# Linear attention beside a gated feed-forward block: activation loads split and reordered, one mean subtracted by ScalarE, first transposes copied in halves, warm-up matmuls on a constant

## The chip, the cores and the metric

The kernel runs on one core of one Trainium2 chip. The metric is the time of one execution on the device in microseconds (us). Lower is better. Engines are named as in the profile: PE is TensorE, ACT is ScalarE, DVE is VectorE, POOL is GpSimd, and SP is SyncE, which issues the DMA transfers here.

## The reference

The input x has 2048 rows (tokens) of 512 columns in bfloat16. It is normalised per row (mean and variance, no scale or shift), and two branches of the result are added to it:

```python
xn = _layernorm(x)
# A: linear attention, H = 32 heads of 16
q, k, v = split(xn @ wqkv)
phi = lambda z: concat(softmax(z @ w_phi), softmax(-(z @ w_phi)))   # per head, 32 features
kv, z = phi(k)^T v, sum over tokens of phi(k)
A = ((phi(q) kv) / (phi(q) z + 1e-6)) @ wo
# B: gated feed-forward, 1792 hidden
B = ((xn @ w_gate) * (xn @ w_up)) @ w_down
out = x + A + B
```

## The kernel before, in words

The tokens are worked in 16 tiles of 128 rows. SBUF is one array, `arena`, in which names are offsets; PSUM is one array, `ps`, with eight banks of 512 float32 columns.

Each tile of x is centred, transposed so that the 512 columns lie on partitions in four quarters (`xnT`, quarter q), and multiplied by the value weights (`k_pe`) and the key and query weights. The key and query weights are first folded with `w_phi` into `Wp` (`wprime`), for which they are loaded transposed by a DMA (`load_wT`). The feed-forward block is worked in units of 128 hidden columns by 512 tokens (`glu`): four matmuls for the gate, four for the up part, a copy of the gate by ACT and a product by DVE. These units have low priority and fill PE's time between the steps of the attention. At the end `final` multiplies by `w_down` and `wo`, adds x and stores.

**Order of the work.** The code records steps with what they read and write. A list planner (`_order`) then sets the order on each engine from costs and due times written into the code: a DMA has an `at`, the time in ns at which its data counts as landed. Among steps that could start, the earliest goes first, and at equal times the one with the lower number. A step marked `urgent` is taken ahead of others if it can start within a grace (50 ns on PE, 300 ns elsewhere). `_emit_all` writes this fixed order into the engines' queues with semaphore waits. Each queue is worked in order: a step that waits holds up what stands behind it.

**The first 16 us**, where the edit lies. The first four tiles (`RAW = 4`) are only centred before their transpose; their scale is applied later. For each of them:

- `emit_centred(t)` finds the mean and subtracts it. Tiles 0, 2 and 3 do this on DVE: BATCH_NORM_STATS2 (L415), BATCH_NORM_AGGREGATE (L416), subtraction (L430). Tile 1 is in `ACT_MEAN`: its mean comes from an ACT activation with an accumulated sum (L423), and the subtraction stays on DVE (L430). Its variance is found later.
- `emit_T(t)` transposes the tile by four matmuls against the identity into one bank and copies the bank to `xnT` by one ACT activation (`act_op`, L277).
- `emit_root(t)` works the row's scale on POOL.
- `k_pe(t)` multiplies by the value weights: four matmuls of 512 columns, one for each quarter q. They are separate steps for the first four tiles. Quarters 0 and 1 need the first half of the value weights, 2 and 3 the second.

All matmuls are recorded at one line (L297), all plain DMA issues at L165, DMA transposes at L164, and PSUM copies by ACT at L277.

Loads at the start are issued by SP in this order: x tile 0, x tile 1, x tiles 2 and 3 in one transfer, the two halves of the value weights, gate and up weights (first four units), `w_phi`, x tiles 4 to 7, the transposed key weights, and more gate and up weights.

Before the first data is there, PE runs 27 matmuls on a block of zeros that DVE has written (L368, L369) into a bank that nothing reads, and four more behind tile 1's transpose.

Of the kernel before, what the change touches and what calls it, by code (L numbers as in the profile page):

```python
# [5 lines left out]
BF16 = mybir.dt.bfloat16  # L6
F32 = mybir.dt.float32
ACTF = mybir.ActivationFunctionType
# [4 lines left out]
PE, ACT, DVE, POOL, SP = "PE", "ACT", "DVE", "POOL", "SP"  # L13
# [7 lines left out]
NQ = D // 128  # L21
# [160 lines left out]
def bass_parallel_sum__linear_kernel_hedgehog__glu_gated_bilinear__prompt_kernel(  # L182
    nc: bass.Bass,
    A_x: bass.AP,
    A_wqkv: bass.AP,
    A_w_phi: bass.AP,
    A_wo: bass.AP,
    B_x: bass.AP,
    B_w_gate: bass.AP,
    B_w_up: bass.AP,  # L190
    B_w_down: bass.AP,
    out: bass.AP,
):
    with ExitStack() as es:
        _build(nc, es, A_x, A_wqkv, A_w_phi, A_wo, B_w_gate, B_w_up, B_w_down, out)


def _build(nc, es, A_x, A_wqkv, A_w_phi, A_wo, B_w_gate, B_w_up, B_w_down, out):
# [59 lines left out]
    def sbv(name, lo, n):  # L258
        off = layout[name] + lo
        return arena[:, off:off + n]  # L260

    def sbf(name, lo_f32, n_f32):
        off = layout[name]
        return arena[:, off:off + 2 * (lo_f32 + n_f32)].bitcast(F32)[:, lo_f32:lo_f32 + n_f32]

    def bank(b, lo=0, n=512):
        return psum[:, b * 512 + lo: b * 512 + lo + n]

    sc = _Sched(nc)


    def act_op(out_ap, in_ap, func=ACTF.Copy, scale=1.0, bias=None, prio=None):
        def fn(e):
            kw = {}
            if bias is not None:
                kw["bias"] = bias
            return e.activation(out=out_ap, in_=in_ap, func=func, scale=scale, **kw)  # L277
        r = [in_ap]
        if isinstance(scale, bass.AP):
            r.append(scale)  # L280
        if isinstance(bias, bass.AP):
            r.append(bias)
        return sc.step(ACT, fn, reads=r, writes=[out_ap], cost=(50.0 if str(in_ap.tensor.name) == "ps" else 95.0) + 0.833 * in_ap.free_size(),
                       lat=180.0, prio=prio)

    def dve(fn, reads, writes, n, rate=1.0, fixed=65.0, prio=None):
        return sc.step(DVE, fn, reads=reads, writes=writes, cost=fixed + rate * n / 0.96, lat=150.0, prio=prio)
# [4 lines left out]
    def mms(items, prio=None, cold=False):  # L292

        def fn(e):
            ins = None
            for o, l, r, a, z in items:
                ins = e.matmul(o, lhsT=l, rhs=r, start=a, stop=z)  # L297
            return ins
        reads = []
        writes = []  # L300
        c = 0.0
        for o, l, r, a, z in items:
            reads += [l, r]
            writes.append(o)
            c += max(25.0, o.free_size() / 2.4 + 2.3) * (1.92 if cold else 1.0)
        return sc.step(PE, fn, reads=reads, writes=writes, cost=c, lat=260.0, prio=prio)
# [12 lines left out]
    def x_tile(t):  # L319
        return sbv("x", t * 512, 512)  # L320

    xnT_v = sbv("xnT", 0, NQ * S_TOK).rearrange("p (q s) -> p q s", q=NQ)
# [5 lines left out]
    wv_v = sbv("wv", 0, NQ * 512).rearrange("p (q j) -> p q j", q=NQ)  # L328
# [7 lines left out]
    def load_x(on, t0, n, at):  # L336
        return sc.dma(on, sbv("x", t0 * 512, n * 512).rearrange("p (t d) -> p t d", t=n),
                      x_flat[t0 * 128:(t0 + n) * 128, :].rearrange("(t p) d -> p t d", p=128), at=at)

    def load_w(on, dst, src, at, issue=500.0):  # L340
        return sc.dma(on, dst, src, at=at, issue=issue)
# [5 lines left out]
    def load_gu(on, f0, n, at):  # L347
        return [load_w(on, v[:, :, f0 * 128:(f0 + n) * 128],
                       src[:, f0 * 128:(f0 + n) * 128].rearrange("(q p) f -> p q f", p=128), at)
                for v, src in ((wg_v, B_w_gate), (wu_v, B_w_up))]  # L350

    load_x(SP, 0, 1, 2950.0)
    load_x(SP, 1, 1, 3400.0)
    load_x(SP, 2, 2, 4700.0)
    wv_loads = [load_w(on, wv_v[:, 2 * h:2 * h + 2, :],
                       A_wqkv[h * 256:(h + 1) * 256, 1024:1536].rearrange("(q p) j -> p q j", p=128), at)
                for on, h, at in ((SP, 0, 5700.0), (SP, 1, 6600.0))]
    load_gu(SP, 0, 4, 9300.0)
    sc.dma(SP, wphi_v, bass.AP(tensor=A_w_phi.tensor, offset=A_w_phi.offset, ap=[[16, 128], [2048, NQ], [1, 16]]),
           at=10900.0)  # L360
# [3 lines left out]
    load_gu(SP, 9, 5, 22300.0)  # L364


    zero = sbv("tree", 0, 128)
    dve(lambda e: e.memset(zero, 0.0), [], [zero], 128)  # L368
    mms([(bank(7, 0, 128), zero, zero, True, True)] * 27, cold=True)  # L369


    def c_fn(e):
# [30 lines left out]
    mv_v = sbf("mv", 0, NT * 2).rearrange("p (t k) -> p t k", t=NT)  # L403
# [10 lines left out]
    def emit_moments(t):  # L414
        dve(lambda e: e.bn_stats(stats_v[:, t, 0:6], x_tile(t)), [x_tile(t)], [stats_v[:, t, 0:6]], 512)  # L415
        dve(lambda e: e.bn_aggr(mv_v[:, t, :], stats_v[:, t, 0:6]), [stats_v[:, t, 0:6]], [mv_v[:, t, :]], 6)  # L416

    def emit_centred(t):

        reads = [x_tile(t)]  # L420
        if t in ACT_MEAN:
            mean = lnt_v[:, 2, 8 + t:9 + t]
            sc.step(ACT, lambda e: e.activation(out=xn_tile(t), in_=x_tile(t), func=ACTF.Copy, scale=1.0 / 512.0,  # L423
                                                accum_out=mean),
                    reads=[x_tile(t)], writes=[xn_tile(t), mean], cost=720.0, lat=180.0)
            reads.append(xn_tile(t))
        else:
            mean = mv_v[:, t, 0:1]
            emit_moments(t)
        dve(lambda e: e.tensor_scalar(out=xn_tile(t), in0=x_tile(t), scalar1=mean, scalar2=None,  # L430
                                      op0=ALU.subtract), reads + [mean], [xn_tile(t)], 512, rate=0.5)

# [3 lines left out]
    def emit_root(t):  # L436
        pool(lambda e: e.tensor_scalar(out=veps(t), in0=mv_v[:, t, 1:2], scalar1=1e-5, scalar2=None, op0=ALU.add),
             [mv_v[:, t, :]], [veps(t)], 1)
        pool(lambda e: e.tensor_tensor(out=rstd_v[:, t, 0:1], in0=veps(t), in1=mhalf[:, 0:1], op=ALU.pow),
             [veps(t), mhalf], [rstd_v[:, t, 0:1]], 1, rate=155.0, fixed=400.0)  # L440
# [22 lines left out]
    def xn_tile(t):  # L463
        return sbv("xn", (t % 4) * 512, 512)
# [4 lines left out]
    def next_a():  # L469
        b = a_bank[0] % a_banks[0]  # L470
        a_bank[0] += 1
        return b

    def emit_T(t):
        b = (5, 6, 7, 4)[t] if t < RAW else next_a()
        mms([(bank(b, q * 128, 128), xn_tile(t)[:, q * 128:(q + 1) * 128], ident, True, True) for q in range(NQ)],
            cold=t < 2)
        act_op(xnT_v[:, :, t * 128:(t + 1) * 128], bank(b).rearrange("p (q s) -> p q s", q=NQ))

    def emit_xn(t):  # L480
        dve(lambda e: e.tensor_scalar(out=xn_tile(t), in0=x_tile(t), scalar1=mv_v[:, t, 0:1],  # L481
                                      scalar2=rstd_v[:, t, 0:1], op0=ALU.subtract, op1=ALU.mult),
            [x_tile(t), mv_v[:, t, 0:1], rstd_v[:, t, 0:1]], [xn_tile(t)], 512, rate=0.5)
        if t >= 4:
            sc.dma(SP, xnT_v[:, :, t * 128:(t + 1) * 128], xn_tile(t), transpose=True, issue=1250.0, land=3200.0,
                   at=36000.0 + 1300.0 * (t - 8) if t >= 8 else 23600.0 + 550.0 * (t - 4))
            return
        emit_T(t)
# [63 lines left out]
    def k_pe(t):  # L552
        b = next_a()
        items = group(bank(b), [(xnT(q, t * 128, 128), wv_v[:, q, :]) for q in range(NQ)])
        if t < RAW:
            for item in items:
                mms([item])
        else:
            mms(items)
        act_op(vext_all[:, t, :, 0:64], bank(b).rearrange("p (c j) -> p c j", c=8), scale=scale_of(t))  # L560
# [166 lines left out]
    for t in range(RAW):  # L727
        first = len(sc.steps)
        emit_centred(t)
        emit_T(t)  # L730
        for st in sc.steps[first:]:
            st.urgent = True
        if t == 1:
            mms([(bank(7, 0, 128), zero, zero, True, True)] * 4, cold=True).deps.append(sc.by_eng[PE][-2])
        if t in ACT_MEAN:
            emit_moments(t)
        emit_root(t)
        k_pe(t)
# [192 lines left out]
```

## Time and profile before

| What | Value |
|---|---|
| Median of 3 runs | 219.8 us (219.64 to 220.88) |
| The profiled execution | 219.75 us |
| Its span (first to last instruction) | 218.5 us |
| PE busy | 213.9 us, 98% of the span |
| DVE busy | 193.0 us, 88% |
| ACT busy | 115.8 us, 53% |
| POOL busy | 10.7 us, 5% |
| DMA packets' share of 16 engines | 40.4% |

The span leaves out what lies around the instructions, 1.25 us here. A busy PE need not be at its peak, since matmuls are pipelined and the profile models their ends. From one matmul's start to the next one's start is the measure of its pace. Idle time of an engine that does not set the end costs nothing.

### The profile page before, as it was taken

The numbers are of one execution on the slowest core, as the hardware profiler recorded it, in microseconds if no ns is written. First come the engines' busy times: TensorE is split into PE (matmuls) and PEld (weight loads), VectorE is DVE, ScalarE is ACT, GpSimd is POOL, SyncE is SP. The second block draws the span as 40 slices with busy tenths as digits, with TensorE's granted clock in tenths as the row PEclk, the third lists the DMA queues.
The fourth block names the chain that finished last, engine by engine and source line by source line (L and its number), as shares of the span: only waits on it lengthen the run. The fifth ranks groups of instructions, "written<-read, shape, count | busy, mean of one in ns | idle before, by whom it ended". The sixth has DMA issues, their size and how long they took to land.

```text
span 218.5 us, 3596 instructions
## 1 busy us (share of the span) xinstructions
PE 213.9 (98%) x1290; PEld 105.0 (48%) x1313; DVE 193.0 (88%) x549; ACT 115.8 (53%) x191; POOL 10.7 (5%) x29
## 2 busy tenths in 40 slices
PE   7999999999999999999999999999999999999996
PEld 7444444444445544444445544444544444454454
DVE  4577999999999389999998899999999999999532
ACT  4658987538443599965553687553444353121000
POOL 4532000010002000000000000000000000000000
DMA  6999540025900440000000002273456548546931
GB/s 172 316 238 354 100 172 4 0 52 147 329 3 13 85 99 0 0 0 3 0 0 1 3 0 48 48 99 74 96 116 128 106 110 106 123 111 126 139 76 48
DMA packets 47458, 19.91 MB, mean 91 GB/s; under 512 B 37456, under 2 KB 47440, under 8 KB 47440
## 3 DMA queue, kind: packets, MB, share of 16 engines
q1 hardware_dynamic: 47440, 19.69, 40.4%
q8 instruction: 10, 0.16, 0.3%
q14 instruction: 8, 0.07, 0.1%
HBM read 8.67 MB, written 2.10 MB: 49 GB/s over the span
## 4 chain that ended last, share of the span: by engine, by line
PE 95%; DMA 2%; issue 1%; SPq 1%; ACT 1%; DVE 0%
PE ps L297 95%; DMA arena<-in_A_wqkv_dram 2%; SPq L165 1%; ACT arena L277 1%; DVE arena L703 0%
## 5 line engine op out<-in xcount | busy, mean ns | idle before, releaser
L297 PE MATMUL ps<-arena 128*128 128x512 bf16 (+4 forms) x1290 | 213.9, 327 | 2.8 <-DVE arena L368 1.0
L297 PEld LDWEIGHTS ps<-arena 128*128 128x128 bf16 (+1 forms) x1313 | 105.0, 99 | 111.5 <-issue 1.1
L277 ACT ACTIVATE arena<-ps 128x512 bf16<-128x512 f32 (+1 forms) x136 | 71.8, 583 | 47.1 <-PE ps L297 40.2
L277 ACT ACTIVATE arena<-arena 128x1024 bf16<-128x1024 bf16 (+1 forms) x40 | 38.5, 977 | 30.1 <-DVE arena L528 29.9
L542 DVE TENSOR_TENSOR arena<-arena 128x512 f32<-128x512 bf16 (+3 forms) x128 | 48.8, 392 | 0.2
L598 DVE TENSOR_TENSOR arena<-ps,arena 128x512 bf16<-128x512 f32 x56 | 38.3, 683 | 5.8 <-PE ps L297 4.7
L522 DVE TENSOR_TENSOR arena<-arena 128x64 bf16<-128x64 bf16 (+3 forms) x128 | 31.5, 271 | 3.8 <-ACT arena L277 3.5
L528 DVE TENSOR_TENSOR arena<-arena 128x1024 bf16<-128x1024 bf16 x32 | 21.7, 680 | 0.1
L703 DVE TENSOR_TENSOR arena<-ps,arena 128x512 bf16<-128x512 f32 (+2 forms) x13 | 8.3, 642 | 7.1 <-PE ps L297 7.1
L574 DVE TENSOR_TENSOR arena<-arena 128x1024 bf16<-128x1024 bf16 x16 | 10.8, 678 | 0.0
L277 ACT ACTIVATE arena<-ps,arena 128x512 bf16<-128x512 f32 x12 | 7.8, 681 | 2.6 <-PE ps L297 2.6
L571 DVE RECIPROCAL arena<-arena 128x64 bf16<-128x64 f32 x16 | 8.7, 544 | 0.0
L675 DVE TENSOR_TENSOR arena<-ps,arena 128x512 bf16<-128x512 f32 x12 | 8.1, 678 | 0.1
L452 DVE BATCH_NORM_STATS2 arena<-arena 128x6 f32<-128x512 bf16 x12 | 8.0, 684 | 0.0
L667 DVE RECIPROCAL arena<-ps 128x32 f32<-128x32 f32 x16 | 5.6, 349 | 1.8 <-PE ps L297 1.8
L654 DVE TENSOR_TENSOR arena<-arena 128x512 bf16<-128x512 bf16 x16 | 6.6, 415 | 0.0
L651 DVE RECIPROCAL arena<-arena 128x32 f32<-128x32 f32 x16 | 5.4, 338 | 0.0
L481 DVE TENSOR_SCALAR arena<-arena 128x512 bf16<-128x512 bf16 x12 | 4.3, 400 | 0.7 <-POOL arena L460 0.7
L415 DVE BATCH_NORM_STATS2 arena<-arena 128x6 f32<-128x512 bf16 x4 | 2.8, 690 | 2.1 <-DMA arena<-in_A_x_dram 2.0
L458 POOL TENSOR_SCALAR arena<-arena 128x4 f32<-128x4 f32 x3 | 0.8, 257 | 52.2 <-DVE arena L454 52.2
L460 POOL TENSOR_TENSOR arena<-arena 128x4 f32<-128x4 f32 x3 | 3.1, 1049 | 0.2
L700 DVE SCALAR_TENSOR_TENSOR arena<-ps,arena 128x512 bf16<-128x512 f32 x4 | 3.0, 748 | 0.1
(29 smaller groups left out, 24.4 us busy)
## 6 DMA issues: line engine op xcount, KB each, us to landing
out_dram<-arena SPq DMA_DIRECT2D x15, 128.0 KB, 1.9
arena<-in_B_w_down_dram SPq DMA_DIRECT2D x1, 1792.0 KB, 7.5
arena<-in_B_w_gate_dram SPq DMA_DIRECT2D x2, 640.0 KB, 6.6
arena<-in_B_w_up_dram SPq DMA_DIRECT2D x2, 640.0 KB, 7.8
arena<-in_A_x_dram SPq DMA_DIRECT2D x1, 1024.0 KB, 5.7
arena<-arena SPq DMA_TRANSPOSE x44, 2.6
arena<-in_A_wqkv_dram SPq DMA_DIRECT2D x2, 256.0 KB, 3.9
arena<-in_B_w_gate_dram SPq DMA_DIRECT2D x1, 512.0 KB, 5.7
```

The source lines that it names most:

```text
L277: return e.activation(out=out_ap, in_=in_ap, func=func, scale=scale, **kw)
L297: ins = e.matmul(o, lhsT=l, rhs=r, start=a, stop=z)
L452: dve(lambda e, t=t: e.bn_stats(stats_v[:, t, 0:6], x_tile(t)), [x_tile(t)], [stats_v[:, t, 0:6]], 512)
L522: dve(lambda e, dst=dst, src=src, k=k: e.tensor_tensor(out=dst, in0=src[:, :, 0:k], in1=src[:, :, k:2 * k], op=ALU.max), [src], [dst], 16 ...
L528: dve(lambda e: e.tensor_tensor(out=p4, in0=p4, in1=src[:, :, None, :].to_broadcast([128, 16, 16, 4]), op=ALU.subtract), [pst, src], [pst] ...
L542: dve(lambda e, dst=dst, src=src, k=k: e.tensor_tensor(out=dst, in0=src[:, :, 0:k], in1=src[:, :, k:2 * k], op=ALU.add), [src[:, :, 0:2 * ...
L571: dve(lambda e: e.reciprocal(out=rs, in_=sm), [sm], [rs], 64, rate=6.0)
L574: dve(lambda e: e.tensor_tensor(out=e4, in0=e4, in1=r4[:, :, None, :].to_broadcast([128, 16, 16, 4]), op=ALU.mult), [ek_v[:, t, :], rs], [ ...
L598: dve(lambda e: e.tensor_tensor(out=dst, in0=bank(bu), in1=gr, op=ALU.mult), [bank(bu), gr], [dst], 512, prio=-1.0)
L654: dve(lambda e: e.tensor_tensor(out=e1, in0=e1, in1=rs[:, :, None, :].to_broadcast([128, 8, 16, 4]), op=ALU.mult), [e1, rs], [e1], 512, ra ...
L675: dve(lambda e: e.tensor_tensor(out=o4, in0=n4, in1=w4, op=ALU.mult), [nd[:, :, 0:64], w], [o], 512)
L703: dve(lambda e: e.tensor_tensor(out=og, in0=ob, in1=xs, op=ALU.add), [ob, xs], [og], c1 - c0, prio=-2.0)
```

## The change

- x tiles 2 and 3 are loaded by two transfers. Tile 3's is issued between the two halves of the value weights. The due times of these loads are changed.
- For tile 1, ACT accumulates the negative mean and then adds it by a second activation (Identity with the mean as bias) instead of DVE's subtraction.
- Each of the first four transposed banks is copied by two activations of 256 columns instead of one of 512.
- The matmuls of the start multiply a constant of ones, made at the program's start, instead of zeros that DVE writes. There are 32 instead of 27 ahead of the first transpose, and two behind each of the transposes of tiles 0 and 1 instead of four behind tile 1's.

```diff
+    def load_v(h, at):
+        return load_w(SP, wv_v[:, 2 * h:2 * h + 2, :],
+                      A_wqkv[h * 256:(h + 1) * 256, 1024:1536].rearrange("(q p) j -> p q j", p=128), at)
+
     load_x(SP, 0, 1, 2950.0)
     load_x(SP, 1, 1, 3400.0)
-    load_x(SP, 2, 2, 4700.0)
-    wv_loads = [load_w(on, wv_v[:, 2 * h:2 * h + 2, :],
-                       A_wqkv[h * 256:(h + 1) * 256, 1024:1536].rearrange("(q p) j -> p q j", p=128), at)
-                for on, h, at in ((SP, 0, 5700.0), (SP, 1, 6600.0))]
+    load_x(SP, 2, 1, 4000.0)
+    load_v(0, 5250.0)
+    load_x(SP, 3, 1, 5500.0)
+    load_v(1, 6900.0)
     load_gu(SP, 0, 4, 9300.0)
...
-    zero = sbv("tree", 0, 128)
-    dve(lambda e: e.memset(zero, 0.0), [], [zero], 128)
-    mms([(bank(7, 0, 128), zero, zero, True, True)] * 27, cold=True)
+    one = nc.const_aps.tensor(1.0, [128, 128], BF16)
+    mms([(bank(7, 0, 128), one, one, True, True)] * 32, cold=True)
...
         if t in ACT_MEAN:
             mean = lnt_v[:, 2, 8 + t:9 + t]
-            sc.step(ACT, lambda e: e.activation(out=xn_tile(t), in_=x_tile(t), func=ACTF.Copy, scale=1.0 / 512.0,
+            sc.step(ACT, lambda e: e.activation(out=xn_tile(t), in_=x_tile(t), func=ACTF.Copy, scale=-1.0 / 512.0,
                                                 accum_out=mean),
                     reads=[x_tile(t)], writes=[xn_tile(t), mean], cost=720.0, lat=180.0)
-            reads.append(xn_tile(t))
-        else:
-            mean = mv_v[:, t, 0:1]
-            emit_moments(t)
+            sc.step(ACT, lambda e: e.activation(out=xn_tile(t), in_=x_tile(t), func=ACTF.Identity, bias=mean),
+                    reads=[x_tile(t), xn_tile(t), mean], writes=[xn_tile(t)], cost=522.0, lat=180.0)
+            return
+        mean = mv_v[:, t, 0:1]
+        emit_moments(t)
         dve(lambda e: e.tensor_scalar(out=xn_tile(t), in0=x_tile(t), scalar1=mean, scalar2=None,
                                       op0=ALU.subtract), reads + [mean], [xn_tile(t)], 512, rate=0.5)
...
-        act_op(xnT_v[:, :, t * 128:(t + 1) * 128], bank(b).rearrange("p (q s) -> p q s", q=NQ))
+        for q in range(0, NQ, 2):
+            act_op(xnT_v[:, q:q + 2, t * 128:(t + 1) * 128], bank(b, q * 128, 256).rearrange("p (q s) -> p q s", q=2))
...
-        if t == 1:
-            mms([(bank(7, 0, 128), zero, zero, True, True)] * 4, cold=True).deps.append(sc.by_eng[PE][-2])
+        if t < 2:
+            mms([(bank(7, 0, 128), one, one, True, True)] * 2, cold=True).deps.append(sc.by_eng[PE][-2])
```

## The prediction

> **What bounds the kernel now.** I read the page first, then the chain that ended last, then the timeline of the first 16 us engine by engine, then single records where a merged row hides steps.
>
> ```profile
> PE 213.9 (98%) x1290; PEld 105.0 (48%) x1313; DVE 193.0 (88%) x549; ACT 115.8 (53%) x191; POOL 10.7 (5%) x29
> PE   7999999999999999999999999999999999999996
> PE 95%; DMA 2%; issue 1%; SPq 1%; ACT 1%; DVE 0%
> ```
>
> TensorE (PE) works without a hole from the second slice to the last, and 95% of the chain is PE. All that the change touches lies in the first slice and a half. So it can act on the end only by how much earlier PE reaches the same point of its own work. That head start is kept as long as no load comes too late for it.
>
> ```profile
> 2.69 4.46 DMA arena<-in_A_wqkv_dram
> 7.16 0.05 issue
> 7.20 0.82 PE ps L297 x3
> 8.02 0.05 issue
> 8.08 6.66 PE ps L297 x33
> 14.74 0.02 issue
> 14.76 0.61 ACT arena L277
> ```
>
> The chain of waits, in order of time: the second half of the value weights (v1) lands at 7.16 and PE starts at 7.20. From there on PE runs through. The matmul before began at 6.707 and had 0.216 to run (49 of these take 10.74 us), so PE stood from 6.92 to 7.20: 0.28 us, its only loss to a load at the start. Later steps with a hole are 0.1 to 0.3 us each and belong to forms the change leaves alone.
>
> ```profile
> 1.03 3.06 PE L297 MATMUL ps<-arena 128*128 128x128 bf16 x27 [1.03 <-DVE arena L368]
> 2.95 0.69 DVE L415 BATCH_NORM_STATS2 arena<-arena 128x6 f32<-128x512 bf16 x1 [1.97 <-DMA arena<-in_A_x_dram]
> 3.39 0.63 ACT L423 ACTIVATE arena<-arena 128x512 bf16<-128x512 bf16 x1 [1.33 <-DMA arena<-in_A_x_dram]
> 3.89 0.68 DVE L430 TENSOR_SCALAR arena<-arena 128x512 bf16<-128x512 bf16 x2
> 4.95 1.08 ACT L277 ACTIVATE arena<-ps 128x512 bf16<-128x512 f32 x2 [0.84 <-PE ps L297]
> 5.64 0.35 DVE L430 TENSOR_SCALAR arena<-arena 128x512 bf16<-128x512 bf16 x1
> 6.49 0.27 PEld L297 LDWEIGHTS ps<-arena 128*128 128x128 bf16 x4 [0.25 <-issue]
> 6.84 0.35 DVE L430 TENSOR_SCALAR arena<-arena 128x512 bf16<-128x512 bf16 x1
> ```
>
> The timeline of the start: 27 fill matmuls until DVE has centred tile 0 (2.95 to 4.25); its transposes T0 at 4.30; T1 at 4.70, right behind; four fills; at 5.70 the first value matmul of tile 0 (k0q0; q is the quarter of the contraction), released by the end of T0's whole copy (4.95 to 5.55) with v0 landed at 5.57; k0q1 at 6.08; T2 at 6.48; k1q0 at 6.71; then the hole. The clock column says 1.00 throughout, but the steps do not: 128 columns take 107 ns up to about 6.45 us and 56 ns after, so **PE runs at half speed until 6.45**.
>
> ```profile
> 0.00:3.40 3.40, 2.37 (x23) 2.37 (x24) 0.56 (x2) 1.30 (x2) 1.53 (x11) 1.00 0.40 95
> 3.40:7.20 3.80, 3.48 (x26) 2.18 (x25) 3.47 (x11) 2.09 (x5) 2.25 (x5) 1.00 0.96 299
> ```
>
> The windows by stage (last two columns: DMA share, GB/s): from 3.4 us on the DMA engines are full. Loads land when their bytes' turn comes, rather than when SP issues them.
>
> **The change, part by part.** (1) Fill on ones: no DVE memset (0.11 us) and no wait for it. The constant is written by 0.46, and ACT and DVE begin at 0.78 and 0.87, so the fills begin between 0.78 and 1.03; I take 0.8, as nothing but the launch holds them. 32 x 107 ns end at 4.22, before T0 at 4.30, where DVE's unchanged chain (2.95, 0.69, 0.18, 0.35) still puts it. Cost and gain of their own: 0 as long as T0 waits for DVE. At the other end, 1.03, they end at 4.45, and T0 is 0.15 later.
>
> (2) Tile 1 by ScalarE. DVE loses one subtract (0.35). ACT gains an Identity with a bias from memory, behind the accumulator's read (end 4.11). No such row exists: Copy from SBUF takes 629 ns, and a scale from memory costs 681 against 605 ns, so I take 0.70 (bounds 0.63 and 1.06, the 1024-column row). It starts at 4.15 and ends at 4.85; ACT's ends reach PE about 0.12 later (5.547 to the weight load at 5.67), so T1 starts at 4.97 instead of 4.70: 0.27 late. In the gap stand the two fills now put behind T0 (4.71 to 4.92), and ACT is free before T0's copy at 4.95. T1 ends at 5.40, its two fills at 5.61. No second table load is priced here: the one load already serves Copy and Exp; if Identity needed its own, that is 1.28 us on ACT, twice.
>
> (3) Copies in halves. ACT rows give 225 ns for 65 columns and 605 for 512, so 256 take 0.39, and neighbours overlap by 0.1. The first half of T0 is there at 5.34 instead of 5.55, the second at 5.62. Four more instructions cost ACT about 0.1 us each; they lie in its idle time (4.8 us of waits for PE in the first 16 us).
>
> (4) Loads. x2 alone is issued at 1.71 as before; 128 KB take 2.1 to land, 256 KB took 3.0, so x2 is there between 3.85 and 4.67; I take 3.9 to 4.1. DVE is free at 4.25, so its stats run from 4.16 to 4.85, the aggregate to 5.07, the subtract to 5.46 (it was 5.99). x3 has the place in the bytes that v0 had, so it lands near 5.6: stats to 6.28, subtract to 6.89. T3 is then not late. v1 and all behind it are issued one issue (0.46 to 0.5) later, with the same bytes ahead.
>
> **The order that follows.** The planner's own costs (used for the order alone, not for any time) put T2 ready 21 ns behind the last fill, inside its 50 ns of grace for urgent steps. So T2 now goes ahead of k0q0. Then come k0q0, k0q1, k1q0, k1q1, k2q0, T3, and only then k0q2, the first that needs v1. On the chip: T2 at 5.61 (DVE ready 5.52) for 0.43 cold, to 6.04; k0q0 cold to 6.46; k0q1 to 6.68; k1q0 to 6.90; k1q1 to 7.11; k2q0 to 7.33; T3 to 7.55; k0q2 at 7.55. Copies: T1's first half 6.04, T2's 6.68; both in time. What now stands behind T2 in PE's queue is k0q0 and with it all value matmuls: with x2 at its late bound, 4.67, T2 waits until 6.08, k0q2 comes at about 7.79, and only 0.07 of the gain is left.
>
> Before, k0q2 stood at 7.20 with less done: k1q1, k2q0 and T3 are 0.216 + 0.216 + 0.224 = 0.656 more. The same point was thus 7.86, and **PE gains 0.31 us**: 0.03 from the start up to k1q0 (6.68 against 6.71) and 0.28 from the hole, if v1 lands by 7.50. It landed at 7.16; with a full issue added, 7.66, the gain is 0.15.
>
> **Does the head start last?** up0 landed at 10.58 and is first used at 11.11: 0.47 of slack. The transposed key weights landed at 13.98 for 14.65: 0.62. The head start of 0.31 fits both, if they land where they did. A whole issue later (11.06) leaves up0's first use no gain. The engines are full, so I take 0 to 0.2 later and keep 0.5 for the range. The sum against the profiled execution: 218.5 of span less 0.31, plus 1.25 outside it, from 219.75 to 219.44. The median of the runs is 219.8, 0.05 above that execution; I forecast **219.4**.
>
> **Rivals.** (a) *The loads behind are late by the added issue.* up0 lands at 11.06, PE waits there, nothing is left: 219.8. For: every load from v1 on is issued 0.5 later. Against: the share of 0.96 and 1.10 of the DMA engines between 3.4 and 14.6 us. (b) *The clock rises earlier.* The fills start 0.25 us sooner and their hole at 4.1 shrinks from 0.4 to 0.1. If the rise comes before T2, T2 and k0q0 save up to 0.43. But up0 caps the total at 0.47: 219.3. Against: before, too, PE was busy from 1.03, and the rise still took until 6.45.
>
> The Trainium skill (TensorE: Matmul & The Clock Gate, Part 1) says that the gate judges free-running windows of about 3.4 us, whatever the kernel's start. By this rule the rise would stay near 6.45 or jump back a window, to an estimated 3.04; it would not creep by 0.25. The trace shows one rise only, so it can't tell these apart; the rule gives case (b) its mechanism, and the same 219.3.
>
> (c) *Slower: v1 is late.* x3 stands ahead of it and the 512 KB gate and up loads follow directly. v1 already took 4.46 us where v0 took 3.4, so newer bytes do delay older ones. Issued at 3.15 with 5.0 (between its own 4.46 and gate's 5.7) it lands at 8.15, PE starts k0q2 at 8.2 against an even point of 7.86: 220.1. It decides from a landing at 7.81 on. Gate's own 5.7 would give 8.85 and 220.8. Against: the bytes ahead of it are the same. (d) *The fills or halves do nothing and the planner's later order differs.* Its estimate of the front moves by 40 ns only (9.64 to 9.60), so most choices stay; one flipped choice costs or saves about one hole of 0.2 to 0.3: 219.2 to 220.3.
>
> **How the numbers follow.** The forecast, 219.3 to 219.7: 0.48. (a) 0.17; (b) 0.10; (c) 0.14; (d) 0.11. The range from 218.8 to 220.6 holds all of these but the ends of (c) and (d), and takes in that the runs before spread from 219.64 to 220.88. A difference of 1%, 2.2 us, is about what a measurement of this kernel can tell from no change; no case reaches it. A gain that large has no source in the first slice and a half (0.03); a loss needs a second table load or a badly changed order late (0.05). Within it: 0.92.
>
> **What would show it.** Right: first fill near 0.8; T0 still at 4.3; T1 near 4.95, after the ACT Identity of some 0.7 us; T2 ahead of the first value matmul; no hole at 7.2; every later matmul about 0.3 us earlier; one table load. Wrong: a hole at k0q2 (then v1), at 10.8 (up0) or 14.4 (key weights); steps of 56 ns before 5.6 (b); or later orders that differ.

## The result and the profile after

The changed kernel takes 220.59 us (median of 22 runs, 219.62 to 220.97), the kernel before 219.95 us (22 runs, 219.47 to 220.88): a ratio of 1.0023, with a 95% interval of 1.0013 to 1.0032. It is **slightly slower**, where 219.4 was forecast. The profiled execution took 220.53 us with a span of 219.3, against 219.75 and 218.5: 0.78 us more.

The page of the changed kernel, busy time and the chain by engine:

```profile
PE 215.5 (98%) x1318; PEld 105.4 (48%) x1318; DVE 192.5 (88%) x547; ACT 116.7 (53%) x196; POOL 10.7 (5%) x29
PE 94%; DMA 3%; SPq 1%; issue 0%; DVE 0%
PE ps L297 94%; DMA arena<-in_B_w_up_dram 3%; SPq L165 1%; DVE arena L708 0%
```

PE is still the bound, but the load in the chain is no longer the value weights. It is the up weights. The same chain in order of time (start, length, what):

```profile
3.65 0.47 SPq L165
4.12 0.04 issue
4.16 7.66 DMA arena<-in_B_w_up_dram
11.83 0.05 issue
11.87 205.57 PE ps L297 x1246
```

The up weights are issued at 4.16 and land at 11.83; PE then runs to the end in one piece. Before, that first up matmul ran at 11.11 (single records). So PE's front is 0.77 us behind there, and the span is 0.8 longer: the whole loss arises before 12 us.

The timeline of PE and ACT at the start shows that the steps ahead of the feed-forward block went as forecast:

```profile
0.82 3.57 PE L297 MATMUL ps<-const-bfloat16-1.0 128*128 128x128 bf16 x32 [0.82 <-PEq L921]
4.14 0.72 ACT L429 ACTIVATE arena<-arena 128x512 bf16<-128x512 bf16 x1
4.22 0.61 PE L297 MATMUL ps<-arena 128*128 128x128 bf16 x4
4.92 0.61 PE L297 MATMUL ps<-arena 128*128 128x128 bf16 x4
5.53 4.23 PE L297 MATMUL ps<-arena 128*128 128x128 bf16 x24
```

Fills from 0.82, T0 at 4.22, ACT's Identity of 0.72, T1 at 4.92, and T2 at 5.53 ahead of the value matmuls, which then run without a hole up to 9.6. Then come two holes:

```profile
8.95 0.81 PE L297 MATMUL ps<-arena 128*128 128x512 bf16 x3
10.35 1.04 PE L297 MATMUL ps<-arena 128*128 128x512 bf16 x4 [0.59 <-DMA arena<-in_B_w_gate_dram]
11.87 1.47 PE L297 MATMUL ps<-arena 128*128 128x512 bf16 x6 [0.48 <-DMA arena<-in_B_w_up_dram]
```

The last value matmul starts at 9.38, so the first gate matmul could have started at 9.60; before, it started at 10.24. PE had a **head start of 0.64 us**. From start to start, PE lost 0.75 us to the gate weights and 0.65 to the up weights: 0.64 - 0.75 - 0.65 = -0.76, the measured loss.

The DMA issues (KB, us to landing) and the windows of both kernels, each time the changed one first (last two columns of the windows: DMA share, GB/s):

```profile
arena<-in_B_w_gate_dram SPq DMA_DIRECT2D x1, 512.0 KB, 6.7
arena<-in_B_w_up_dram SPq DMA_DIRECT2D x1, 512.0 KB, 7.7
```

```profile
arena<-in_B_w_gate_dram SPq DMA_DIRECT2D x1, 512.0 KB, 5.7
arena<-in_B_w_up_dram SPq DMA_DIRECT2D x1, 512.0 KB, 6.9
```

```profile
5.00:6.50 1.50, 1.50 (x14) 1.17 (x14) 1.31 (x4) 1.46 (x6) 1.00 (x3) 1.00 0.58 170
```

```profile
5.00:6.50 1.50, 1.50 (x11) 0.80 (x9) 1.43 (x4) 1.03 (x2) 0.74 (x3) 1.00 0.93 257
7.20:10.30 3.10, 3.04 (x17) 1.56 (x19) 1.19 (x5) 2.28 (x5) 1.43 (x4) 1.00 1.10 330
```

Gate and up took 6.7 and 7.7 us to land, where they took 5.7 and 6.9. They were issued 0.45 later and landed 1.37 and 1.25 later (10.31 and 11.83). Between 5.0 and 6.5 us the transfers ran at 170 GB/s in the changed kernel. Before, they ran at 257 there and at 330 later. So the engines had not been full before either: a share of 0.93 went with 257 GB/s.

### The profile page after: what moved, and what is told of

It is laid out like the page before. It is cut to its first block, busy times and chain, and to the rows that moved or that the text cites. A ratio compares the mean times of both kernels' runs of the same rounds, so it can differ in the third digit from the quotient of the medians.

```text
span 219.3 us, 3632 instructions
## 1 busy us (share of the span) xinstructions
PE 215.5 (98%) x1318; PEld 105.4 (48%) x1318; DVE 192.5 (88%) x547; ACT 116.7 (53%) x196; POOL 10.7 (5%) x29
## 3 DMA queue, kind: packets, MB, share of 16 engines
HBM read 8.67 MB, written 2.10 MB: 49 GB/s over the span
## 4 chain that ended last, share of the span: by engine, by line
PE 94%; DMA 3%; SPq 1%; issue 0%; DVE 0%
PE ps L297 94%; DMA arena<-in_B_w_up_dram 3%; SPq L165 1%; DVE arena L708 0%
## 5 line engine op out<-in xcount | busy, mean ns | idle before, releaser
L297 PE MATMUL ps<-arena 128*128 128x512 bf16 (+5 forms) x1282 | 212.0, 328 | 1.1 <-DMA arena<-in_B_w_gate_dram 0.6
L297 PEld LDWEIGHTS ps<-arena 128*128 128x128 bf16 (+1 forms) x1282 | 101.7, 98 | 111.1 <-DMA arena<-in_B_w_gate_dram 1.1
L277 ACT ACTIVATE arena<-ps 128x512 bf16<-128x512 f32 (+2 forms) x140 | 72.0, 570 | 47.6 <-PE ps L297 39.6
L297 PE MATMUL ps<-const-bfloat16-1.0 128*128 128x128 bf16 x36 | 4.4, 313 | 0.8 <-PEq L921 0.8
L297 PEld LDWEIGHTS ps<-const-bfloat16-1.0 128*128 128x128 bf16 x36 | 3.9, 149 | 0.8 <-issue 0.8
```

## The experiments

The landings and starts below are single records of the profiled executions, one for each kernel, while each ratio, to the kernel before on the same chip, comes from 9 to 22 executions of the kernel. "Ahead" counts the transfers that SP issues before the gate weights. First product: the start of DVE's first gate-times-up product, which waits for the first up block.

| Kernel | Ahead | Gate issued, landed | Up landed | First product | Span | Ratio (95%) |
|---|---|---|---|---|---|---|
| before | 5 | 3.21, 8.93 | 10.58 | 12.17 | 218.5 | 1 |
| changed | 6 | 3.65, 10.31 | 11.83 | 12.95 | 219.3 | 1.0023 (1.0013 to 1.0032) |
| e1 loads alone | 6 | 3.64, 10.45 | 11.96 | 13.08 | 219.4 | 1.0035 (1.0022 to 1.0048) |
| e2 changed, old loads | 5 | 3.21, 9.34 | 10.85 | 12.07 | 218.4 | 0.9987 (0.9974 to 1.0000) |
| e4 fill alone | 5 | 3.19, 8.96 | 10.59 | 11.71 | 218.0 | 0.9992 (0.9974 to 1.0010) |
| e5 ACT edits alone | 5 | 3.21, 9.23 | 10.73 | 11.85 | 218.2 | 0.9995 (0.9971 to 1.0019) |
| e3 x 3 ahead | 6 | 3.64, 9.00 | 10.85 | 11.97 | 218.3 | 1.0008 (0.9990 to 1.0026) |
| g1 pair between | 5 | 3.19, 9.10 | 10.79 | 13.50 | 219.8 | 1.0037 (1.0018 to 1.0056) |
| g2 x 3 behind | 6 | 3.68, 10.30 | 11.79 | 13.94 | 219.9 | 1.0016 (0.9997 to 1.0036) |
| h1 value weights whole | 5 | 3.13, 8.45 | 10.14 | 12.69 | 219.0 | 1.0055 (1.0030 to 1.0081) |
| h7 x 0 and 1 joint | 5 | 3.26, 8.47 | 10.59 | 13.91 | 220.3 | 1.0070 (1.0051 to 1.0090) |
| h8 before, x 2 and 3 apart | 6 | 3.64, 10.55 | 12.03 | 13.15 | 219.5 | 1.0028 (0.9999 to 1.0058) |
| k1 before, v1 in two | 6 | 3.68, 9.89 | 11.46 | 12.58 | 218.9 | 1.0023 (1.0007 to 1.0039) |
| h3 before, gate held | 5 | 3.55, 9.77 | 11.25 | 12.37 | 218.7 | 1.0013 (0.9995 to 1.0032) |
| h5 before, held longer | 5 | 4.36, 8.39 | 10.39 | 11.56 | 218.0 | 0.9984 (0.9961 to 1.0006) |
| k2 changed, held | 6 | 4.27, 10.72 | 12.15 | 13.28 | 219.6 | 1.0012 (0.9997 to 1.0027) |
| h2 x 3 by ACT | 5 | 3.18, 8.47 | 10.51 | 12.16 | 218.5 | 1.0018 (1.0001 to 1.0034) |

Span less first product is 206.3 to 206.5 in 18 of the 20 profiles (the two others are g2 and b2, where PE waits for the key weights before they are folded). **What a kernel gains or loses here is settled by about 15 us**; an order that differs later moves nothing.

### Which part of the change

The loads alone, on the kernel before:

```diff
-    load_x(SP, 2, 2, 4700.0)
-    wv_loads = [load_w(...) for on, h, at in ((SP, 0, 5700.0), (SP, 1, 6600.0))]
+    load_x(SP, 2, 1, 4000.0)
+    load_v(0, 5250.0)
+    load_x(SP, 3, 1, 5500.0)
+    load_v(1, 6900.0)
```

> The kernel before with the change of the loads alone (x tiles 2 and 3 apart, tile 3 between the value weights' halves). Theory L (the new loads make the gate and up weights land late, whatever else is edited): gate lands near 10.3 and up near 11.8 us as in the changed kernel, PE stands before the first gate or up matmuls, the time is 0.4 to 0.8 us above before (ratio 1.002 to 1.0035). Theory O (the other edits slow the transfers, by more traffic or an earlier clock): gate and up land near 8.9 and 10.6 as before, and the time is 0 to 0.3 us below before. Theory S (landings scatter from run to run by themselves): landings anywhere, ratio within 0.999 to 1.001.

Theory L held: 1.0035, gate at 10.45, up at 11.96. PE's waits between 7 and 13 us in this kernel:

```profile
PE ps L297 <- DMA arena<-in_B_w_gate_dram: 0.5, 1, 0.5
PE ps L297 <- DMA arena<-in_B_w_up_dram: 0.5, 1, 0.5
```

Both holes of the changed kernel are there without any other edit. The converse, the changed kernel with the loads of before:

```diff
-    load_x(SP, 2, 1, 4000.0)
-    load_v(0, 5250.0)
-    load_x(SP, 3, 1, 5500.0)
-    load_v(1, 6900.0)
+    load_x(SP, 2, 2, 4700.0)
+    wv_loads = [load_w(...) for on, h, at in ((SP, 0, 5700.0), (SP, 1, 6600.0))]
```

> The changed kernel with the loads of before (x tiles 2 and 3 in one transfer, then the two halves of the value weights), all other edits kept. Theory L: gate lands near 8.9 and up near 10.6, no hole before the first gate matmuls, PE's front ahead by what up0 allows, 0.3 to 0.47 us, ratio 0.998 to 0.9985. Theory O: gate and up near 10.3 and 11.8, time as the changed kernel's, ratio 1.002. Theory S: ratio within 0.999 to 1.001.

0.9987, and its chain is one piece of PE from the first value matmul on:

```profile
5.90 0.13 issue
6.03 210.53 PE ps L297 x1274
```

The loss is gone, so the loads are its whole cause. The gain left, 0.13%, has an interval that ends at 1. The fill alone and the ACT edits alone:

```diff
-    mms([(bank(7, 0, 128), zero, zero, True, True)] * 27, cold=True)
+    mms([(bank(7, 0, 128), one, one, True, True)] * 32, cold=True)
...
-        if t == 1:
-            mms([(bank(7, 0, 128), zero, zero, True, True)] * 4, cold=True).deps.append(sc.by_eng[PE][-2])
+        if t < 2:
+            mms([(bank(7, 0, 128), one, one, True, True)] * 2, cold=True).deps.append(sc.by_eng[PE][-2])
```

> The kernel before with the fill edit alone (32 matmuls on the constant, two behind each of the first two transposes). Theory L: landings as before, gate 8.9, up 10.6; the hole for the second value half stays at about 7.2, so the time moves by what the clock does alone: ratio 0.998 to 1.000. If the clock rises before 6 us as in the changed kernel's profile, the first value matmuls take less time and the hole before the second value half grows by as much. Theory O: gate and up land a microsecond later than before, ratio 1.001 to 1.003.

```diff
+            sc.step(ACT, lambda e: e.activation(out=xn_tile(t), in_=x_tile(t), func=ACTF.Identity, bias=mean),
+                    reads=[x_tile(t), xn_tile(t), mean], writes=[xn_tile(t)], cost=522.0, lat=180.0)
...
-        act_op(xnT_v[:, :, t * 128:(t + 1) * 128], bank(b).rearrange("p (q s) -> p q s", q=NQ))
+        for q in range(0, NQ, 2):
+            act_op(xnT_v[:, q:q + 2, t * 128:(t + 1) * 128], bank(b, q * 128, 256).rearrange("p (q s) -> p q s", q=2))
```

> The kernel before with the two ACT edits alone (tile 1's subtraction by ACT, copies in halves). Loads as before: v1 near 6.3 to 7.2, gate 9, up 10.6 to 10.9. The first half copies let the first value matmul start at most 0.2 us sooner, but T1 is 0.27 later with four fills behind it, so the front moves by less than 0.2 either way: ratio 0.999 to 1.001. A ratio below 0.998 would make these edits the source of the gain with the loads of before.

0.9992 and 0.9995, both intervals across 1, landings as before: neither edit harms, and neither alone shows a gain. In both profiles PE waits for the up weights by 0.16 and 0.19 us: once the front is earlier, their landing near 10.6 is the cap, as the slack of 0.47 in the prediction said.

### Order, number or size of the transfers

Tile 3 apart but ahead of both halves; then tiles 2 and 3 in one transfer between the halves; then tile 3 behind both. All on the changed kernel; the lines shown take the place of its loads of tile 2, tile 3 and the value weights:

```diff
+    load_x(SP, 2, 1, 4000.0)
+    load_x(SP, 3, 1, 4700.0)
+    load_v(0, 5500.0)
+    load_v(1, 6900.0)
```

> The changed kernel with x tile 3 still apart but issued ahead of both halves of the value weights: the same number of issues as in the changed kernel, the order of bytes of before. If the added issue alone makes the loads behind it late (theory L1), gate lands after 10 and up after 11.5, ratio 1.001 to 1.003. If tile 3 between the halves is what does it (theory L2), gate lands near 8.9 to 9.4, up near 10.6 to 11.1, ratio 0.998 to 1.000.

```diff
+    load_v(0, 4700.0)
+    load_x(SP, 2, 2, 5500.0)
+    load_v(1, 6600.0)
```

> All edits of the changed kernel, but x tiles 2 and 3 in one transfer and that transfer between the halves of the value weights: as many issues as before, an x transfer between two weight transfers. Theory B (an x transfer between the halves is what makes the loads behind late): gate lands after 10, up after 11.5, ratio 1.001 or more. Theory N (it takes the added issue as well): gate near 9, up near 10.6 to 10.9, ratio 0.998 to 1.000. Under both, x tile 2 lands near 5.4 instead of 4, so T2 and the value matmuls behind it start about 1 us later, which the wait for the gate weights may hide.

```diff
+    load_x(SP, 2, 1, 4000.0)
+    load_v(0, 5250.0)
+    load_v(1, 6400.0)
+    load_x(SP, 3, 1, 6900.0)
```

> The changed kernel with x tile 3 issued behind both halves of the value weights: the same number and sizes of transfers as in the changed kernel, none between the halves. Theory B: gate lands near 9 to 9.4, up near 10.6 to 10.9, ratio 0.998 to 1.000. Rival W (any x transfer issued after a weight transfer does it): gate after 10, up after 11.5, ratio 1.001 to 1.003.

The first seemed to say that the place between the halves does it: gate at 9.00. The second refutes that: an x transfer between the halves, five ahead, gate at 9.10. (Its own loss has another source: PE stands 1.2 us for the second half of the value weights, until 7.69, and the chain then runs from the x tiles' landing at 5.53 through DVE, POOL and ACT to PE at 10.70.) The third has none between and six ahead: 10.30. The first kernel's twelve times spread from 219.18 to 220.83, and the profiled one, 219.56, is among the short ones; so its other executions may well have landed later, which no profile shows. Two more at five ahead (the first again on the changed kernel), and two at six that leave the order of the bytes as it was before:

```diff
+    load_x(SP, 2, 1, 4000.0)
+    load_x(SP, 3, 1, 4700.0)
+    load_w(SP, wv_v, A_wqkv[:, 1024:1536].rearrange("(q p) j -> p q j", p=128), 6600.0)
```

> The changed kernel with x tiles 2 and 3 apart, both ahead of the value weights, and the value weights in one transfer: five transfers ahead of gate as before, gate issued near 3.2. Theories T and X both: gate near 9, up near 10.6 to 10.9. Value matmuls can't start before the whole lands, near 6.3 to 7.2, so PE stands 0.5 to 1 us there but has four tiles' value work, 3.45 us, behind it: first gate matmul near 10.2 to 10.9, ratio 0.998 to 1.001. If gate still lands after 10, small x transfers by themselves do it.

On the kernel before, with the changed order and tiles 0 and 1 joint (these lines are all of its loads of x tiles 0 to 3 and of the value weights):

```diff
+    load_x(SP, 0, 2, 3400.0)
+    load_x(SP, 2, 1, 4000.0)
+    load_v(0, 5250.0)
+    load_x(SP, 3, 1, 5500.0)
+    load_v(1, 6900.0)
```

> The kernel before with the changed order (tile 3 between the value weights' halves), but x tiles 0 and 1 in one transfer, so that gate is issued near 3.2 as before. Theory T: gate near 8.5 to 9.3, up near 10.1 to 10.9. Theory B2 (tile 3 between or behind the halves does it at any issue time): gate after 10, up after 11.5. Tile 0 lands with tile 1, near 3.4 instead of 2.9, so T0 starts 0.5 later and the front can be up to 0.5 later than before: ratio 0.999 to 1.003 under T, 1.003 to 1.005 under B2.

On the kernel before, tiles 2 and 3 apart and nothing else:

```diff
-    load_x(SP, 2, 2, 4700.0)
+    load_x(SP, 2, 1, 4000.0)
+    load_x(SP, 3, 1, 4700.0)
```

> The kernel before with x tiles 2 and 3 apart, both ahead of the value weights, nothing else edited: one issue more, gate issued near 3.65, order of bytes as before. Theory T: gate after 9.7, up after 11.1, ratio 1.001 to 1.0035. Theory B2: gate near 9, up near 10.6 to 10.9, ratio 0.999 to 1.001.

On the kernel before, the x loads untouched and the second half of the value weights cut:

```diff
-                for on, h, at in ((SP, 0, 5700.0), (SP, 1, 6600.0))]
+                for on, h, at in ((SP, 0, 5700.0),)]
+    for q in (2, 3):
+        load_w(SP, wv_v[:, q:q + 1, :], A_wqkv[q * 128:(q + 1) * 128, 1024:1536]...., 6600.0)
```

> The kernel before with the second half of the value weights in two transfers of 128 KB, one for each quarter; the x loads as before. So six transfers stand ahead of gate on SP's queue instead of five, with the bytes and the order of before. Theory X (the sixth transfer ahead makes the loads behind late, whatever it carries): gate after 10, up after 11.5, ratio 1.002 to 1.004. Theory Y (it takes x tiles in small transfers): gate near 9, up 10.6 to 10.9, ratio 0.999 to 1.001.

Five ahead: gate lands at 8.45 and 8.47, with small x transfers and even with tile 3 between the halves; both kernels take longer than the one before for other reasons (value matmuls from 7.09; T0 at 5.00). Six ahead: 10.55 and 9.89. **Gate is late with a sixth transfer ahead, whether that one carries an x tile or a part of the value weights, and wherever it stands**; the order alone does not do it. This holds for six of the seven profiles with six ahead. Tile 3 ahead of both halves is the exception, by its landing and by its ratio (1.0008, across 1). The gap is narrow too: the latest landing with five ahead is 9.77, the earliest of the six late ones 9.89.

### The time of issue

A sixth transfer also makes gate's issue 0.45 later. Two kernels hold gate and all loads behind it, with nothing added to the kernel before, until DVE's first statistics end, and until tile 0 is centred; a third does the latter to the changed kernel:

```diff
+    held = len(sc.by_eng[SP])
     load_gu(SP, 0, 4, 9300.0)
...
         emit_centred(t)
+        if t == 0:
+            for ld in sc.by_eng[SP][held:]:
+                ld.deps.append(sc.by_eng[DVE][-3])    # the two later kernels: [-1]
```

> The kernel before, with nothing changed but that SP holds the gate weights' load and those behind it until DVE's first statistics end (3.64 us), so that gate is issued near 3.67 instead of 3.2 with no transfer added. Theory T (the later issue by itself makes gate and up land 1.2 to 1.4 us later): gate lands after 10, up after 11.5, ratio 1.002 to 1.004. Theory X (it takes the added transfer in the queue): gate lands at 8.9 to 9.4, up at 10.6 to 11.1, ratio 0.999 to 1.001.

> The kernel before with gate's load and those behind it held until DVE has centred tile 0 (4.25 us): gate issued near 4.28, 1.07 later than before, no transfer added. Held by 0.34 it landed 0.84 later and up 0.67 later. Theory T (landing follows the issue, and by more than the delay, because the transfer engines run dry meanwhile): gate near 11 to 11.5, up near 12.5 to 13, first up matmul at up's landing, time 1.4 to 1.9 us above before, ratio 1.006 to 1.009. Theory X (the added transfer does it, the delay of 0.34 was scatter): gate by 10, up by 11.6, ratio below 1.003.

> The changed kernel, its six transfers ahead of gate kept, with gate's load and those behind it held until DVE has centred tile 0 (4.17 us, issue near 4.25). If the harm comes from gate being queued close behind the others (holding kept the landing early in the kernel before: 8.4 and 10.4), gate lands near 8.4 to 9.2 and up near 10.3 to 10.9, PE keeps 0.3 to 0.5 us of its head start, ratio 0.997 to 0.999. If six transfers ahead are late however gate is spaced, gate lands after 10 and up after 11.5, ratio 1.002 to 1.004.

Held by 0.34, gate landed 0.84 later, which spoke for theory T. Held by 1.15 it landed **earlier** than without a hold, and T fell. The DMA issues of the kernel held longer, and of the one with x tiles 2 and 3 apart:

```profile
arena<-in_B_w_gate_dram SPq DMA_DIRECT2D x1, 512.0 KB, 4.0
arena<-in_B_w_up_dram SPq DMA_DIRECT2D x1, 512.0 KB, 5.6
```

```profile
arena<-in_B_w_gate_dram SPq DMA_DIRECT2D x1, 512.0 KB, 6.9
arena<-in_B_w_up_dram SPq DMA_DIRECT2D x1, 512.0 KB, 7.9
```

The same 512 KB take 4.0 us behind five transfers issued up to 3.2 us, and 6.9 behind six. With six, the same hold did not help in the profile (10.72). But that execution was the longest of twelve, which spread from 219.29 to 220.87; their ratio of 1.0012 (0.9997 to 1.0027) is below the changed kernel's, and whether holding helps there is not decided.

**What is late is a part of the transfer.** The trace has sixteen landing counts for each transfer, and the landings above are the last of the sixteen. For the gate weights (us):

| Kernel | Ahead | 8th count | 12th | 15th | 16th (landed) |
|---|---|---|---|---|---|
| before | 5 | 7.82 | 8.03 | 8.67 | 8.93 |
| h3 before, gate held | 5 | 7.73 | 8.30 | 8.66 | 9.77 |
| changed | 6 | 8.40 | 9.12 | 10.17 | 10.31 |
| e1 loads alone | 6 | 8.10 | 8.28 | 8.42 | 10.45 |
| k2 changed, held | 6 | 8.64 | 8.87 | 8.96 | 10.72 |
| e3 x 3 ahead | 6 | 7.98 | 8.28 | 8.34 | 9.00 |

In all 17 kernels of the first table half of the counts are in by 7.5 to 8.6 us. What differs is the tail: a single count in e1 and k2, the last four in the changed kernel (9.96 to 10.31). A tail exists with five ahead too (h3). The next load keeps it: in e1 the up weights' fifteenth count comes at 10.48 and the last at 11.96. Meanwhile later loads pass: ten of the up weights' counts come before gate's last one in the changed kernel and fifteen in k2, none in the kernel before.

The bytes say the same. Windows from the start to the usual landing of gate, the kernel before, then tile 3 behind, there also to its own landing, then the changed kernel:

```profile
0.00:8.93 8.93, 7.52 (x56) 5.47 (x58) 5.22 (x16) 4.77 (x8) 4.97 (x19) 1.00 0.77 229
```

```profile
0.00:8.93 8.93, 8.11 (x64) 6.10 (x64) 4.79 (x14) 5.91 (x12) 4.91 (x19) 1.00 0.73 223
0.00:10.30 10.30, 9.00 (x68) 6.41 (x68) 4.79 (x14) 7.15 (x15) 5.19 (x19) 1.00 0.78 239
```

```profile
0.00:8.93 8.93, 8.11 (x65) 6.35 (x66) 4.78 (x14) 5.93 (x14) 5.21 (x19) 1.00 0.66 197
```

229 x 8.93 is 2.04 MB, and gate had landed; with tile 3 behind, 223 x 8.93 is 1.99 MB, and it had not; it did at 239 x 10.30 = 2.46 MB. Up to the end of gate 1.57 MB are asked for. So there the lower rate between 5.0 and 6.5 us is not needed for a late landing. In the changed kernel itself less had moved by then, 197 x 8.93 = 1.76 MB, so a lower rate comes on top.

**What stays open** is why a sixth transfer ahead lengthens the tail. A tail that the next load keeps agrees with one or a few of the 16 engines lagging behind the rest, but the counts do not name their engines, and which one lags and why was not shown.

### Versions made from this

Tile 3 issued by ACT, so that SP keeps five ahead:

```diff
+    load_x(ACT, 3, 1, 4400.0)
```

> The changed kernel with x tile 3 issued by ACT at the start, so that SP has one issue less ahead of the gate weights (gate near 3.2). Theory T: gate near 9, up near 10.6 to 10.9, ratio 0.997 to 0.999. Theory X (six transfers ahead of gate, whoever issues them): gate after 10, up after 11.5, ratio 1.001 to 1.003. A price that may show: x tile 3's bytes beside tile 0's make T0 later, by up to 0.3 us.

Gate lands at 8.47, as theory T expected, though a sixth transfer exists: in this profile one on another engine's queue does no harm to gate. But tile 0 is late:

```profile
3.37 0.69 DVE L418 BATCH_NORM_STATS2 arena<-arena 128x6 f32<-128x512 bf16 x1 [3.37 <-DMA arena<-in_A_x_dram]
4.73 0.40 PE L297 MATMUL ps<-arena 128*128 128x128 bf16 x4 [0.34 <-DVE arena L434]
```

It lands at 3.35 instead of 2.92, T0 starts at 4.73, T2 waits for its tile until 6.32, and the ratio is 1.0018. The price named in advance, larger than named, ate the gain. Next, the first gate and up weights in two pairs, with the loads of before, with the changed loads, and with tile 3 issued by ACT behind a POOL step that ends at 2.15:

```diff
-    load_gu(SP, 0, 4, 9300.0)
+    load_gu(SP, 0, 2, 8700.0)
+    load_gu(SP, 2, 2, 10600.0)
```

> The changed kernel with the loads of before, and the first gate and up weights loaded in two pairs of 256 columns instead of one pair of 512 (two more issues on SP). If PE's front is capped by up0's landing (10.6 to 10.9 so far), the first up block lands near 9.8, the cap moves forward by up to 0.7 us and the time falls below that of the kernel with the loads of before: 218.9 to 219.4, ratio 0.995 to 0.998. If rows of 512 bytes or two more transfers slow the queue, gate or up land as late as before or later: ratio 0.999 to 1.002.

> The changed kernel, its loads kept, with the first gate and up weights in two pairs of 256 columns. If the harm is that gate0 and up0 land late, smaller first transfers take it away: first pair by 9.6 and 10.2 at the latest, ratio 0.996 to 0.999. If the second pair or the key weights are late instead, a hole opens at the third unit or before the folded weights (PE idle near 12 to 15 us), ratio 1.000 to 1.003.

```diff
+    x3 = load_x(ACT, 3, 1, 4700.0)
...
-    pool(c2_fn, [ident, bind8], [ident, bind8], 300)
+    x3.deps.append(pool(c2_fn, [ident, bind8], [ident, bind8], 300))
```

> The changed kernel with x tile 3 issued by ACT once POOL has made the identity (2.15 us), so that SP's later issues keep their times of before, and the first gate and up weights in two pairs. T0 as before (x tile 0 alone at first); first pair by 8 and 9 us, v1 near 7; PE's first gate matmul near 9.4 to 9.7 with no hole there, first up matmul near 10.3 to 10.6, time 218.9 to 219.3, ratio 0.996 to 0.998. If the key weights' landing (14.0) is then late for the folding, up to 0.3 us come back as a hole near 14.

With the loads of before: 219.51 against 220.0 us, 0.9978 (0.9965 to 0.9990), in time 0.1 us above what was expected. The first pair lands by 8.8 and PE has no hole in the window (to 13 us) from the value weights on:

```profile
7.00 6.22 PE L297 MATMUL ps<-arena 128*128 128x512 bf16 x31 [0.15 <-DMA arena<-in_A_wqkv_dram]
```

With the changed loads: 1.0018 (1.0004 to 1.0032). The first pair is in time (9.62), but the key weights land at 15.18, and PE loses 0.91 us there:

```profile
15.22 2.04 PE L297 MATMUL ps<-arena 64*128 64x64 bf16 x38 [0.74 <-DMA arena<-in_A_wqkv_dram]
```

The pairs are not what makes them late: with the loads of before and pairs the key weights landed at 14.02, in the changed kernel at 15.17 without pairs, and in the kernel before at 13.98. Everything behind the sixth transfer is late, and the hole has only moved on. With tile 3 by ACT: 219.5 us against 219.9, 0.9980 (0.9962 to 0.9998), in time 0.2 us above what was expected. So two versions are slightly faster than the kernel before, and the changed kernel is slightly slower than it; the two versions are not told apart.

## Why the prediction was wrong

**Right.** Fills from 0.82 (0.8 forecast). ACT's Identity 0.72 us, ending at 4.865 (0.70, 4.85), with one table load. Half copies 0.38 (0.39). x2 at 3.97 (3.9 to 4.1), x3 at 5.45 (5.6). The order: T2 ahead of the first value matmul and k0q2 behind T3, exactly as derived. v1 at 7.17, so rival (c) named the wrong load. T1 at 4.92 instead of 4.97, since ACT's end reached PE in 0.05, not 0.12. The later order, rival (d), moved nothing.

**Too small.** The head start was 0.64, not 0.31: the clock rose near 5.8 instead of 6.45, so T2 and k0q0 were faster, rival (b). It ends at the loads, as the cap said. The runs do not show that the change moved the rise. With the new fill it fell between 3.5 us (tile 3 ahead of both halves) and about 6.5 (loads of before), with the old one between under 4.4 (held longer) and 10.0 (tiles 0 and 1 joint). The rule that the prediction cited from the Trainium skill (TensorE: Matmul & The Clock Gate, Part 1) is windows of about 3.4 us that run free of the kernel's start. By it the rise could scatter by one window, an estimated 3.4 us, and not only stay or jump by a whole one, as the prediction took it. The 3 us of the new fill agree with that; the 10.0 does not come out of it alone. There PE stood for 0.9 us before T0, and whether that is the reason was not shown.

**The step that failed** is the one under "Does the head start last?": the engines are full, so the loads behind v1 would be 0 to 0.2 later. Gate was 1.37 and up 1.25 later. Rival (a) had the place and the direction, but it took the added issue, 0.46 to 0.5, as the most that could be added. Two errors stand behind this. The share of 0.96 was read as full, but its row also said 299 GB/s, against 330 a few us later in the same trace. And the delay was taken as an issue passed on, while h5 shows that a later issue by itself need cost nothing (1.15 later, landed at 8.39). In its place the runs show that the loss goes with the number of transfers ahead on the queue, through the last one to four of the sixteen landing counts; why stays open.

**Luck.** The measured 220.59 lies at the edge of the stated 218.8 to 220.6. The range reached so far because of the cases (c) and (d), a late v1 and another order later, which did not come about, and because of the scatter of the runs before; it did not foresee this loss.

## What to carry to other kernels

Cutting one load of a queue into two, so that its first part lands earlier, can cost the loads behind it more than one issue. Check the landing of the next two or three loads against the time at which they are first used, not only the load that is waited for now. Full transfer engines are read from the GB/s against the trace's own highest value, not from the share. When a critical load has less slack than the head start that is planned (here 0.47 us), make it smaller first (here: two pairs of 256 columns).

## What the runs showed of the hardware that was not expected

- With six transfers ahead on SP's queue the 512 KB gate load landed at 9.9 to 10.7 us in six of seven profiles, with five at 8.4 to 9.8 in all ten, whatever was in them; issued 1.15 us later behind five, it took 4.0 us instead of 5.7.
- A late load is late by its tail: with the new loads alone, fifteen of gate's sixteen landing counts were in by 8.42 us and the last came at 10.45.
- Later loads pass earlier ones on one queue: fifteen of the up weights' counts came before the last of the gate weights' in the changed kernel with gate held (10.72).
- TensorE's half-speed phase ended anywhere from 3.5 to 10.0 us after the start, in kernels whose first matmul differed by 0.2 us.
